# Column sums of a gate's normalisation: from a float32 product of 8 columns to a product of 16 split columns

## The chip, the cores and the metric

The kernel runs on one core of a Trainium2 chip. The metric is the device time of one execution in microseconds (us). The engines are PE (TensorE; its weight loads are listed apart, as PEld), DVE (VectorE), ACT (ScalarE), POOL (GpSimd) and SP (SyncE, which issues the transfers here).

## What is computed

Three stages follow one another: an attention through packed keys, a gated two-layer network, and a network of eight experts. The change lies in the weights that the third stage gives its experts. `P` has one row for each of 2304 tokens and one column for each of 8 experts; eight times its rows and then its columns are scaled to fixed sums.

```python
def _moe2_ref(x, w_gate, w1, w2):
    N, D = x.shape
    E = w_gate.shape[1]
    logits = x @ w_gate
    logits = logits - logits.max()
    P = np.exp(logits)
    for _ in range(8):
        P /= P.sum(1, keepdims=True) + 1e-09
        P /= P.sum(0, keepdims=True) + 1e-09
        P *= N / E
    out = np.zeros((N, D), dtype=np.float32)
    for e in range(E):
        h = np.maximum(x @ w1[e], 0.0)
        ye = h @ w2[e]
        out += P[:, e:e + 1] * ye
    return out
```

## The kernel before

The third stage is cut into groups of tokens. The first group has 256 tokens, and its work runs in 16 steps (two halves of the inner width for each expert), some 370 to 551 us into the span. While it runs, the normalisation is worked off beside it, in small pieces: `sinkhorn` (L1225) is a generator, and the loop of the first group (L1475) calls it once in each half step, behind the half step's second product. The order on PE, DVE and ACT is the order in which the code is written.

A step `s` has two halves, `j = 0` and `j = 1`, and each goes as follows. PE computes the first layer of half the inner width (`up0`: four wide products at L1026, four of 256 columns at L1029, and both once more; tile `u`). ACT copies a part of the result (L1035) and DVE adds the two parts (L1036, tile `us`). The result is split into a rounded part (ACT, L1042) and a rest (DVE, L1043, tile `h`). PE computes the second layer of the step before for 128 of the tokens (`down0`, L1058, 12 products of 512 columns, tile `d`). Beside that, weights are split in the same way: ACT rounds a block (L870), and DVE subtracts the rounded part from the raw one (L872), in j = 0 for the first layer of the next step (`w1l`), in j = 1 for the second layer of this step (`w2l`). Each split makes two blocks in a half. The second `w2l` block of a step is first read by the eighth of the 12 products of the following half, since the products take `w2h`, `w2l`, `w2h` for each of four pieces of the inner width and the second block starts with the third piece. A raw block is loaded anew once DVE has subtracted it.

An iteration of the normalisation takes two such pieces. Behind the half j = 0, DVE forms the row sums' reciprocals, scales `P`, and sums each column over the 18 tokens of a partition (L1269 to L1275, result `csum`, 128 partitions by 8). Behind the half j = 1, one product of `csum` with a matrix of ones adds up the partitions (L1278; all in float32; tile `cs`), and DVE adds a small constant, takes the reciprocal and scales `P` (L1280 to L1282), and then begins the next iteration's row sums (L1269). All eight iterations lie between 396 and 481 us. From the step of expert 4 on, DVE also adds up the weighted outputs (L1070, L1071, L1078), and in part of the stage it prepares the tokens of the second group (L976, L987).

Of the kernel before, what the change touches and what calls it, by code (L numbers as in the profile page):

```python
# [9 lines left out]
F32 = mybir.dt.float32  # L10
F32R = mybir.dt.float32r
# [3 lines left out]
ALU = mybir.AluOpType  # L15
AX = mybir.AxisListType
# [4 lines left out]
NE, FF2 = 8, 1024  # L21
# [5 lines left out]
EPS = 1e-9  # L27
# [77 lines left out]
def fused_kernel(  # L105
# [15 lines left out]
    pe, dve, act = nc.tensor, nc.vector, nc.scalar  # L121

    def pool(name, bufs, **kw):
        st = ExitStack()
        return st.enter_context(tc.tile_pool(name=name, bufs=bufs, **kw)), st

    const, _ = pool("const", 1, side="left"); ctx.enter_context(_)
# [24 lines left out]
    ones = const.tile([128, 128], F32, name="ones")  # L152
# [1072 lines left out]
    def sinkhorn():  # L1225
        lgs = {}
        for hh in (1, 0):
            ps = p3.tile([128, 512], F32, tag="y", name=f"lg{hh}")
            q0, nj, w = GATE[hh]
            for k in range(4):  # L1230
                for j in range(nj):
                    q = q0 + w * j
                    pe.matmul(ps[32 * j:32 * j + 32, :w], wg[:, k, :],  # L1233
                              x2[q // SB][k][:, q % SB:q % SB + w],
                              start=(k == 0), stop=(k == 3), tile_position=(0, 32 * j))
            lg = st["S"].tile([128, 2, 256], F32, tag="S", name=f"lgs{hh}").rearrange("p i n -> p (i n)")[:32 * nj, :w]
            dve.tensor_copy(lg, ps[:32 * nj, :w])
            lgs[hh] = lg
        yield
        Pt = const.tile([128, NE, 18], F32, name="P")  # L1240
        P = Pt.rearrange("p e t -> p t e")
        prob["P"] = P
        for hh in range(2):
            ps = p3.tile([128, 512], F32, tag="y", name=f"lt{hh}")
            q0, nj, w = GATE[hh]
            t0, nc_, m = q0 // 128, w // 128, 32 * nj
            for c in range(nc_):
                pe.transpose(ps[:, m * c:m * c + m], lgs[hh][:, 128 * c:128 * c + 128],
                             ident[:m, :m])
            dve.tensor_copy(  # L1250
                Pt[:, :, t0:t0 + nj * nc_].rearrange("p e (j c) -> p j c e", c=nc_),
                ps[:, :m * nc_].rearrange("p (c j e) -> p j c e", c=nc_, j=nj)[:, :, :, :NE])
        pm = const.tile([128, 1], F32, name="pm")
        dve.tensor_reduce(pm, Pt, AX.XY, ALU.max)
        yield
        ps = p3.tile([128, 512], F32, tag="y", name="gm")
        pe.transpose(ps[:1, :128], pm, ident)
        gm = const.tile([1, 1], F32, name="gmx")
        dve.tensor_reduce(gm, ps[:1, :128], AX.X, ALU.max, negate=True)
        yield  # L1260
        ps = p3.tile([128, 512], F32, tag="y", name="gb")
        pe.matmul(ps[:, :1], ones[:1, :], gm, start=True, stop=True)
        gb = const.tile([128, 1], F32, name="gb")
        dve.tensor_copy(gb, ps[:, :1])
        act.activation(Pt, Pt, AF.Exp, bias=gb)
        rsum = const.tile([128, 18], F32, name="rsum")
        csum = const.tile([128, NE], F32, name="csum")
        for it in range(8):
            dve.tensor_reduce(rsum, P, AX.X, ALU.add)  # L1269
            if it:  # L1270
                yield
            dve.tensor_scalar_add(rsum, rsum, EPS)
            dve.reciprocal(rsum, rsum)
            dve.tensor_tensor(P, P, rsum.unsqueeze(2).to_broadcast([128, 18, NE]), op=ALU.mult)
            dve.tensor_reduce(csum, Pt, AX.X, ALU.add)  # L1275
            yield
            ps = p3.tile([128, 512], F32, tag="y", name=f"cs{it}")
            pe.matmul(ps[:, :NE], ones, csum, start=True, stop=True)  # L1278
            rc = const.tile([128, NE], F32, tag="rc", bufs=2, name="rc")
            dve.tensor_scalar_add(rc, ps[:, :NE], EPS)  # L1280
            dve.reciprocal(rc, rc)
            dve.scalar_tensor_tensor(P, P, float(NT) / NE,  # L1282
                                     rc.unsqueeze(1).to_broadcast([128, 18, NE]),
                                     op0=ALU.mult, op1=ALU.mult)
        yield
        ps = p3.tile([128, 512], F32, tag="y", name="pt")
        Pf = Pt.rearrange("p e t -> p (e t)")
        pe.transpose(ps[:, :128], Pf[:, :128], ident)
        pe.transpose(ps[:16, 128:256], Pf[:, 128:], ident)
        t = st["cp"].tile([128, NB], F32, tag="cp", name="pts")  # L1290
        dve.tensor_copy(t[:, :128], ps[:, :128])
        dve.tensor_copy(t[:16, 128:256], ps[:16, 128:256])
        rows = pd.rearrange("e (t c) -> (e t) c", c=128)
        nc.sync.dma_start(rows[:128], t[:, :128])
        nc.sync.dma_start(rows[128:], t[:16, 128:256])
# [157 lines left out]

    with tc.manual_schedule(engines={mybir.EngineType.PE, mybir.EngineType.DVE, mybir.EngineType.Activation}):
        sk = sinkhorn()
        next(sk)
        for g in (1, 2):
# [116 lines left out]
```

## Time and profile before

| | before |
|---|---|
| time, median of 3 runs (lowest to highest) | 1777.64 us (1777.58 to 1777.78) |
| the profiled execution, its own time | 1776.45 us |
| span of the profiled execution | 1774.7 us |
| PE busy | 1760.6 us, 99% |
| PE weight loads busy | 1492.9 us, 84% |
| DVE busy | 1453.0 us, 82% |
| ACT busy | 1086.2 us, 61% |
| granted clock of TensorE | 1.00 of full speed |

The span is the time from the first instruction of the execution to the last; the device time contains 1.75 us more. The share of DVE is a mean over the whole span, and single stages lie far above it.

### The profile page before, as it was taken

Reading aid. Unit: us, or ns where it says so; the run is one execution under the profiler, and the core shown is the slowest. Engines: PE = TensorE matmul, PEld = TensorE weight load, DVE = VectorE, ACT = ScalarE, POOL = GpSimd, SP = SyncE. Lnnn points to the kernel's source line nnn. Section 1 sums busy time; section 2 is a strip of 40 time slices with the busy share of each in tenths; the row PEclk is TensorE's granted clock in tenths of the full one; section 3 lists DMA queues with packets and bytes.
Section 4 is the critical chain, followed back from the end, with each engine's and each line's share of the span. In section 5 each row is a group of like instructions: output and inputs, shape, how many; then the busy total and the mean of one; then the engine's idle time right before and its main releaser. Section 6 shows DMA issues by size and latency. Waiting matters only on the chain.

```text
span 1774.7 us, 24847 instructions
## 1 busy us (share of the span) xinstructions
PE 1760.6 (99%) x9320; PEld 1492.9 (84%) x9320; DVE 1453.0 (82%) x1954; ACT 1086.2 (61%) x1737; POOL 1.0 (0%) x8
## 2 busy tenths in 40 slices
PE   7999999999999999999999999999999999999999
PEld 5999999988888888888888888888888888888887
DVE  7968797668996989998889999887777777777778
ACT  6776675655664666656666666655555555555555
POOL 0000000000000000000000000000000000000000
PEclk9999999999999999999999999999999999999999
DMA  9326776866674755566454555955555444545442
GB/s 377 117 96 223 253 268 255 331 214 188 203 240 150 264 181 177 167 206 208 160 178 167 179 193 201 323 190 172 159 170 168 151 159 143 172 155 172 148 130 95
DMA packets 141000, 341.72 MB, mean 193 GB/s; under 512 B 11840, under 2 KB 49104, under 8 KB 139984
## 3 DMA queue, kind: packets, MB, share of 16 engines
q1 hardware_dynamic: 140880, 340.14, 56.8%
q8 instruction: 73, 1.20, 0.3%
q14 instruction: 47, 0.39, 0.1%
HBM read 256.66 MB, written 83.44 MB: 192 GB/s over the span
## 4 chain that ended last, share of the span: by engine, by line
PE 95%; DMA 2%; DVE 1%; ACT 1%; issue 0%; SPq 0%; DVEq 0%
PE d L1151 34%; PE X L1199 20%; PE Z L1199 10%; PE g2w L709 8%; PE g L616 5%; PE d L1058 5%; PE Y L1199 5%; PE u L1026 3%; PE g L672 3%; PE u L1029 2%; DMA kq<-in_kT_dram 2%; DMA rawout<-in_moe_w_out_dram 1%; PE u L194 1%; PE lg L1233 0%; DVE S L826 0%
## 5 line engine op out<-in xcount | busy, mean ns | idle before, releaser
L145 DVE TENSOR_TENSOR lo<-hb,hi 128x1024 fp32r<-128x1024 f32 x224 | 273.7, 1222 | 32.9 <-ACT hi L144 32.0
L1151 PE MATMUL d<-hi,w2f 128*128 128x512 f32 x896 | 294.2, 389 | 0.0
L1199 PE MATMUL X<-xf,w1l 128*128 128x512 f32 x1152 | 276.9, 389 | 0.0
L144 ACT CAST hi<-hb 128x1024 fp32r<-128x1024 f32 x224 | 235.3, 1051 | 66.7 <-PE d L1151 61.2
L1199 PEld LDWEIGHTS X<-xf,w1l 128*128 128x128 f32 x1152 | 216.2, 188 | 44.9
L1159 ACT COPY M<-d 128x512 f32<-128x512 f32 x235 | 137.9, 589 | 140.2 <-PE d L1151 139.0
L1163 DVE TENSOR_TENSOR M<-d,M 128x512 f32<-128x512 f32 x203 | 139.7, 688 | 99.9 <-PE d L1151 99.9
L1151 PEld LDWEIGHTS d<-hi,w2f 128*128 128x128 f32 x896 | 168.1, 188 | 34.9
L1151 PE MATMUL d<-lo,w2f 128*128 128x512 f32 x448 | 174.3, 389 | 0.0
L1151 PE MATMUL d<-hi,w2l 128*128 128x512 f32 x512 | 167.7, 389 | 0.0
L709 PE MATMUL g2w<-ring,woh 128*128 128x384 f32 x576 | 147.0, 335 | 0.2 <-DVE U L581 0.2
L1147 ACT COPY d<-M 128x512 f32<-128x512 f32 x217 | 127.7, 589 | 21.6 <-DVE M L1163 20.4
L1151 PE MATMUL d<-hi,w2g 128*128 128x512 f32 x384 | 125.7, 389 | 0.0
L1151 PEld LDWEIGHTS d<-hi,w2l 128*128 128x128 f32 x512 | 96.1, 188 | 20.2 <-ACT d L1147 0.4
L709 PEld LDWEIGHTS g2w<-ring,woh 128*128 128x128 f32 x576 | 102.9, 188 | 4.9 <-issue 3.4
L1206 ACT COPY cp<-X 128x512 f32<-128x512 f32 x128 | 74.5, 583 | 46.5 <-PE X L1199 46.4
L1151 PE MATMUL d<-lo,w2l 128*128 128x512 f32 x256 | 99.6, 389 | 0.0
L1151 PEld LDWEIGHTS d<-lo,w2f 128*128 128x128 f32 x448 | 84.1, 188 | 17.5
L1199 PE MATMUL Y<-xf,w1f 128*128 128x512 f32 x384 | 97.4, 389 | 0.0
L709 PE MATMUL g2w<-ring,wol 128*128 128x384 f32 x288 | 96.2, 334 | 0.0
L144 ACT CAST w1f<-rb 128x512 fp32r<-128x512 f32 x96 | 59.8, 624 | 56.7 <-PE d L1151 42.9
L1199 PE MATMUL Z<-xf,w1l 128*128 128x512 f32 x384 | 92.2, 389 | 0.0
(214 smaller groups left out, 3399.2 us busy)
## 6 DMA issues: line engine op xcount, KB each, us to landing
r<-in_moe_w_dram SPq DMA_DIRECT2D x128, 512.0 KB, 4.1
w1l<-w1d SPq DMA_DIRECT2D x128, 512.0 KB, 4.1
w1d<-po SPq DMA_DIRECT2D x64, 512.0 KB, 4.2
w2d<-w2f SPq DMA_DIRECT2D x64, 512.0 KB, 4.1
w2l<-w2d SPq DMA_DIRECT2D x64, 512.0 KB, 3.5
rb<-in_moe_w_dram SPq DMA_DIRECT2D x96, 256.0 KB, 2.7
sb<-in_moe_w_dram SPq DMA_DIRECT2D x48, 256.0 KB, 2.7
pb<-pd SPq DMA_DIRECT2D x16, 512.0 KB, 5.2
```

The source lines that it names most:

```text
L144: act.copy(out=hi, in_=raw)
L145: eng.tensor_tensor(out=lo, in0=raw, in1=hi.bitcast(F32), op=ALU.subtract)
L616: pe.matmul(ps, lhs[:, fs], rhs, start=(n == 0), stop=(n == 5))
L672: pe.matmul(ps[:, :HS], lhs, rhs, start=(n == 0), stop=(n == 3 * nf - 1))
L709: pe.matmul(ps[:, :TW], lhs[:, f % 2, ds], ring[f // 2][:, 2 * (f % 2) + rhs, q], start=(n == 0 and not on), stop=(n == 11), skip_group_ch ...
L1058: pe.matmul(ps, h[:, l, f % 2, 128 * tt:128 * tt + 128], w[:, f % 2], start=(fh == 0 and n == 0), stop=(fh == 1 and n == 11))
L1147: act.copy(out=ps, in_=m)
L1151: pe.matmul(ps, w[:, l, c, 128 * d:128 * d + 128], r[:, c], start=(n == 0 and not seed), stop=(n == 5), skip_group_check=seed)
L1159: act.copy(out=m, in_=ps)
L1163: dve.tensor_tensor(m, ps, m, op=ALU.add)
L1199: pe.matmul(ps, w[:, l, c, 128 * i:128 * i + 128], x[:, r, c], start=(n == 0 and p in (1, 7)), stop=(n == 5), skip_group_check=p in (2, 6, ...
L1206: act.copy(out=t, in_=ps)
```

## The change

`csum` is split in two: a rounded copy in the type float32r and the rest, both in one tile `cs2` of 16 columns. The matrix of ones is copied once into a float32r tile `onr`. The product then takes `onr` and the 16 columns, in the type in which the neighbouring products `u` and `d` run, and DVE adds the two halves of the result before the constant is added.

```diff
+        cs2 = const.tile([128, 2, NE], F32R, name="cs2")
+        onr = const.tile([128, 128], F32R, name="onr")
+        dve.tensor_copy(onr, ones)
         for it in range(8):
...
             dve.tensor_reduce(csum, Pt, AX.X, ALU.add)
+            dve.tensor_copy(cs2[:, 0], csum)
+            dve.tensor_tensor(cs2[:, 1], csum, cs2[:, 0].bitcast(F32), op=ALU.subtract)
             yield
             ps = p3.tile([128, 512], F32, tag="y", name=f"cs{it}")
-            pe.matmul(ps[:, :NE], ones, csum, start=True, stop=True)
+            pe.matmul(ps[:, :2 * NE], onr, cs2.rearrange("p l e -> p (l e)"), start=True, stop=True)
             rc = const.tile([128, NE], F32, tag="rc", bufs=2, name="rc")
-            dve.tensor_scalar_add(rc, ps[:, :NE], EPS)
+            dve.tensor_reduce(rc, ps[:, :2 * NE].rearrange("p (l e) -> p e l", l=2), AX.X, ALU.add)
+            dve.tensor_scalar_add(rc, rc, EPS)
             dve.reciprocal(rc, rc)
```

On DVE, the second iteration of the normalisation stands as follows before the change, from the column sums of `P` to the reciprocal (`us`, `h` and `w2l` belong to the half step between them):

```order
L1275 TENSOR_REDUCE csum<-P 128x8
L1036 TENSOR_TENSOR us_4817<-u_4800,us_4817 128x512
L872 TENSOR_TENSOR w2l_4794<-r_30_4713,w2h_4793 128x1024
L1043 SCALAR_TENSOR_TENSOR h_4826<-us_4817,h_4826 128x512
L872 TENSOR_TENSOR w2l_4824<-r_31_4736,w2h_4823 128x1024
L1280 TENSOR_SCALAR rc<-cs_4848 128x8
L1281 RECIPROCAL rc<-rc 128x8
```

And with the change (line numbers there are up to six higher):

```order
L1278 TENSOR_REDUCE csum<-P 128x8
L1279 CAST cs_4687<-csum 128x8
L1280 TENSOR_TENSOR cs_4687<-csum,cs_4687 128x8
L1036 TENSOR_TENSOR us_4825<-u_4808,us_4825 128x512
L872 TENSOR_TENSOR w2l_4800<-r_30_4718,w2h_4799 128x1024
L1043 SCALAR_TENSOR_TENSOR h_4834<-us_4825,h_4834 128x512
L872 TENSOR_TENSOR w2l_4832<-r_31_4741,w2h_4831 128x1024
L1285 TENSOR_REDUCE rc<-cs_4856 128x8
L1286 TENSOR_SCALAR rc<-rc 128x8
L1287 RECIPROCAL rc<-rc 128x8
```

Three instructions join each iteration, two ahead of `us` and one behind the second `w2l`; the order of the others stays. On PE the product keeps its place between the last product `d` of one half and the first product `u` of the next. Before:

```order
L1058 MATMUL d_4829<-w2h_4715,h_4718 128x512
L1278 MATMUL cs_4848<-csum,ones 128x8
L1026 MATMUL u_4855<-xs,w1h_4738 128x512 x2
```

And with the change:

```order
L1058 MATMUL d_4837<-w2h_4720,h_4723 128x512
L1283 MATMUL cs_4856<-cs_4687,onr 128x16
L1026 MATMUL u_4864<-xs,w1h_4743 128x512 x2
```

Only the product itself is another one. ACT, POOL and SP have the same instructions in the same order.

## Rows read from the trace of the kernel before

**Rows 1.** The page: span, busy time by engine, chain by engine.
```profile
span 1774.7 us, 24847 instructions
...
PE 1760.6 (99%) x9320; PEld 1492.9 (84%) x9320; DVE 1453.0 (82%) x1954; ACT 1086.2 (61%) x1737; POOL 1.0 (0%) x8
...
PE 95%; DMA 2%; DVE 1%; ACT 1%; issue 0%; SPq 0%; DVEq 0%
```

**Rows 2.** Chain that ended last: start us, us, engine, tile, line, instructions.
```profile
387.35 0.11 PE gm L1257
387.46 0.93 PE u L1026 x4
...
399.10 0.12 PE cs L1278 x2
...
410.43 0.12 PE cs L1278 x2
410.55 1.02 PE u L1026 x4
...
421.88 1.03 PE u L1026 x4
...
489.94 0.91 PE u L1026 x4
...
501.03 0.91 PE u L1026 x4
```

**Rows 3.** Instructions of L1278: count, shortest/median/longest ns, first and last start.
```profile
L1278 PEld LDWEIGHTS cs<-csum,ones x16: 188/188/189, 398.7 to 478.2; 128*128 128x128 f32 x16
L1278 PE MATMUL cs<-csum,ones x16: 172/214/256, 398.9 to 478.3; 128*128 128x8 f32 x16
```

**Rows 4.** Instructions of three DVE lines, columns as in Rows 3.
```profile
L1259 DVE TENSOR_REDUCE gmx<-gm x1: 273/273/273, 388.8 to 388.8; 1x1 f32<-1x128 f32 x1
...
L1275 DVE TENSOR_REDUCE csum<-P x8: 302/303/305, 397.8 to 475.3; 128x8 f32<-128x144 f32 x8
...
L1280 DVE TENSOR_SCALAR rc<-cs x8: 157/160/161, 401.5 to 480.2; 128x8 f32<-128x8 f32 x8
```

**Rows 5.** Timeline of DVE: start us, us, what, [idle before it <- what ended it].
```profile
396.37 0.41 DVE L1269 TENSOR_REDUCE rsum<-P 128x18 f32<-128x144 f32 x1 [1.82 <-ACT P L1265]
396.81 0.18 DVE L1272 TENSOR_SCALAR rsum<-rsum 128x18 f32<-128x18 f32 x1
...
397.79 0.30 DVE L1275 TENSOR_REDUCE csum<-P 128x8 f32<-128x144 f32 x1
398.01 0.68 DVE L1036 TENSOR_TENSOR us<-u,us 128x512 f32<-128x512 f32 x1
...
459.47 0.69 DVE L1036 TENSOR_TENSOR us<-u,us 128x512 f32<-128x512 f32 x1 [0.43 <-ACT us L1035]
...
465.00 0.69 DVE L1036 TENSOR_TENSOR us<-u,us 128x512 f32<-128x512 f32 x1 [0.20 <-ACT us L1035]
...
492.10 1.22 DVE L872 TENSOR_TENSOR w2l<-r,w2h 128x1024 fp32r<-128x1024 f32 x1
...
498.98 0.69 DVE L1036 TENSOR_TENSOR us<-u,us 128x512 f32<-128x512 f32 x1 [0.92 <-ACT us L1035]
```

**Rows 6.** Busy time in two steps: us, PE, PEld, DVE, ACT, POOL, clock, DMA, GB/s.
```profile
407.50:418.80 11.30, 11.30 (x60) 9.60 (x59) 9.27 (x17) 6.60 (x9) 0.00 (x0) 1.00 0.59 189
...
475.30:486.60 11.30, 11.30 (x60) 9.51 (x59) 11.09 (x18) 7.16 (x10) 0.00 (x0) 1.00 0.63 191
```

**Rows 7.** Timeline of PE: the eighth product of one half's 12.
```profile
494.18 0.40 PE L1058 MATMUL d<-w2l,h 128*128 128x512 f32 x1
```

**Rows 8.** Timeline of all engines, at the stage's end, columns as in Rows 5.
```profile
545.69 1.22 DVE L872 TENSOR_TENSOR w2l<-r,w2h 128x1024 fp32r<-128x1024 f32 x1
...
546.96 0.19 PEld L1058 LDWEIGHTS d<-w2l,h 128*128 128x128 f32 x1 [0.39 <-DVE w2l L872]
```

**Rows 9.** Waits of weight loads: who waited for whom, us in total, times, longest.
```profile
PEld d L1058 <- DVE w2l L872: 0.4, 1, 0.4
```

## The prediction

> **What bounds the kernel now.** I read the page first: PE is busy for 1760.6 of 1774.7 us, and 95% of the chain that ended last is PE's [rows 1]. So whatever shortens PE's own work counts in full, and whatever lies on DVE counts only where PE comes to wait for it. The chain in order of time then shows PE's work around the product that is changed. A step without it lasts 501.03 - 489.94 = 11.09 us, a step with it 421.88 - 410.55 = 11.33 us [rows 2]. One product, with all that it costs its neighbours, is therefore worth 0.24 us: 0.12 us under its own name, the rest in the first group of `u` behind it (1.02 us in place of 0.91) [rows 2]. The trace has 16 weight loads and 16 matmuls for the eight products, so each float32 product runs as two passes, each with a load of its own [rows 3]. The third view is DVE's. In a middle step of this stage it has 9.27 us of work in 11.30 us; in the step at 475 us it has 11.09 [rows 6], and from the wait of 0.20 us that ends at 465.00 to the one of 0.92 us that ends at 498.98 it never waits at all [rows 5]. Nearly the same engine load as PE's: this is the stretch in which added DVE work can be seen. The waits of the weight loads show that PE has come to wait for DVE's `w2l` once before, for 0.39 us, at 546.96 [rows 8, 9].
>
> **The change part by part.** *PE, removed.* A two-pass product of few columns costs 0.24 us, so a pass costs 0.12. A row for one pass alone is near: the product `gm` takes 0.11 us, and the `u` behind it 0.93 in place of 0.91, 0.13 in all [rows 2]; that one streams 128 columns, so its price is an upper one for 16. I take 0.12 for the single pass with 16 columns and 0.12 saved in each product, 8 x 0.12 = 0.96 us. The ends are nothing (if the new product costs what the old one did) and 8 x 0.24 = 1.92 us (if it vanished under its neighbours).
>
> *PE, a wait added?* The product now waits for two more DVE instructions. In the first iteration `csum` ends at 397.79 + 0.30 = 398.09 [rows 5] and the product stands in the chain from 399.10 [rows 2]; in the others DVE is done some microseconds ahead, as `csum` belongs to the half before. The two instructions take 0.39 us (next paragraph), so the sum is ready by 398.48. Nothing is queued late.
>
> *DVE, added.* A cast and a subtraction of 128x8 behind `csum`, and behind the product a reduction of 16 columns to 8 from PSUM. The tiny instructions have one row that is almost the same, the addition on 128x8 from PSUM, 160 ns; as upper neighbours there are reductions of 128 and 144 elements, 273 and 303 ns [rows 4]. Between dependent instructions there is a gap of 0.03 us (396.37 + 0.41 = 396.78 to 396.81), and an independent one begins some 0.08 us before the end of the one ahead of it (397.79 + 0.30 = 398.09 against 398.01) [rows 5]. Cast and subtraction, which depend on each other, push `us` back by 0.03 + 0.16 + 0.03 + 0.17 = 0.39 us, as the overlap at the end is there with and without them. The reduction I take at 0.18, between the addition and the longer reductions and nearer the addition, with its gap 0.21. Together e = 0.60 us for an iteration, on DVE 8 x 0.60 = 4.8 us. From both sides e is 0.45 (150 ns each, no gap) to 0.99 (three times 0.30 and a gap). The cast of the ones is one instruction, and it lies in DVE's wait of 1.82 us for the exponential [rows 5]; without that cover it would be one more 0.2 to 0.3 us on DVE, in a step where DVE has 2 us to spare.
>
> *Where DVE's cover ends.* In the middle steps the 11.30 - 9.27 = 2.03 us of idle time [rows 6] hide 0.60 and the 0.12 by which PE gets faster. For the last two iterations it is otherwise. I follow the lag of DVE behind PE, against before. The wait of 0.43 us that ends at 459.47 takes up the reduction and PE's gain of that step (0.21 + 0.12), so the lag is 0 there. The next wait is 0.20, and it has to cover cast and subtraction: 0.39 - 0.20 = 0.19 is left at 465.00. From there nothing is covered: PE's next gain 0.12, reduction 0.21, cast and subtraction 0.39, PE's last gain 0.12, reduction 0.21 make 1.24 us by the `w2l` at 492.10 [rows 5]. In letters this is 2e + 0.04.
>
> *What is late then.* That `w2l` is the second block of its step. It ends at 492.10 + 1.22 = 493.32, and its first reader is the eighth product of the half, at 494.18 [rows 5, 7]. A load can start 0.05 us after the end of the `w2l` it waits for (545.69 + 1.22 = 546.91 to 546.96) [rows 8], and needs some 0.12 us before its product starts (a pass, above). So there are 494.18 - 0.12 - 0.05 - 493.32 = 0.69 us of slack. A lag of 1.24 us exceeds it, and PE waits 1.24 - 0.69 = 0.55 us at that place. After it DVE's lag is down to the 0.69 that was slack, and the wait of 0.92 us that ends at 498.98 takes that up. A raw block is loaded anew when its `w2l` is done, so loads come later by the lag too, but none that PE's next half waits for.
>
> *The sum.* -0.96 + 0.55 = -0.41 us, in letters -0.96 + (2e + 0.04 - 0.69) = 2e - 1.61, with -0.96 as the floor. The profiled execution would go from 1776.45 to 1776.04 and its span from 1774.7 to 1774.3; the median of the runs shown is 1777.64, 1.19 above that execution, and becomes 1777.2. Behind the stage PE's chain goes on to the end, so I let what is gained stay gained.
>
> **The rivals.** *The cover holds.* If e is under 0.33, no wait arises, and the full 0.96 us come out: 1776.7. Against it stands the row of 160 ns for the smallest instruction; for it, that the slack is a difference of stamps of 0.1 us and that some added instructions may overlap. The Trainium skill, "VectorE: DVE Perf Modes", section on the TRN2 errata, gives a vector instruction 58 cycles from SBUF and 120 from PSUM at 0.96 GHz besides its elements: as an estimate by that page cast, subtraction and reduction take 0.07 + 0.07 + 0.14 = 0.28 us, and this rival would be the forecast. The 160 ns for 8 columns from PSUM [rows 4] are above the 133 ns that the same line gives.
>
> *DVE's additions cost more than PE's saving.* Place and mechanism are those of the forecast, the price of the instructions is the higher one. The sum turns at 2e = 1.61, that is at e = 0.81 us; at the upper bound of 0.99 it is +0.37 us: 1778.0. For it speak the reductions of 0.27 and 0.30 us [rows 4], against it that these read 128 and 144 elements where the new ones read 8 and 16.
>
> *The new product is no cheaper.* No row shows a product of 16 columns in float32r. If it costs the 0.24 us of the old one, PE saves nothing, and DVE's lag, now without PE's two gains of 0.12, is 1.00: a wait of 0.31 us, 1777.95.
>
> *Four passes go, not two.* Were the float32 product four passes long, each would be 0.06 us of the 0.24, and one pass would save 0.18: 1.44 us in eight. DVE's lag would be 1.24 + 2 x 0.06 = 1.36, the wait 0.67 and the sum -0.77: 1776.9. The records speak against it, two loads for each product [rows 3]. The Trainium skill, "FP8 and Floating Point Precision", section TensorE Precision Notes, says that true FP32 takes four passes through the array; the trace here shows two records, and the 0.24 us bound both readings.
>
> **How the numbers follow.** Chances: the forecast (some wait, a small gain, 1776.8 to 1777.5) 0.53, the cover holds 0.20, DVE costs more than PE saves 0.13, a product no cheaper 0.06, four passes 0.04, and 0.04 for something that no row shows. All named cases lie between 1776.7 and 1778.0. The executions before spread over 0.2 us among the timed ones, and the profiled one lies 1.2 us below them, so I add half a microsecond at either end: 1776.2 to 1778.5. A measurement of this kernel tells about 0.2% from no change, 3.6 us. Every named case is within that, so the chances are 0.02 faster, 0.96 the same and 0.02 slower, the outer ones for what no row shows.
>
> **What would show it.** The product `cs` appears with 8 loads and 8 matmuls in place of 16 and 16, and the step in the chain lasts 11.21 us in place of 11.33. Cast, subtraction and reduction appear on DVE with some 0.16 to 0.20 us each. Between 465 and 498 us DVE stays without a wait, and in the half at 493 us a weight load of `d` waits for a `w2l` by about half a microsecond. Wrong I would be if `cs` kept two passes, if no wait for `w2l` appeared at 493 us (then the gain is 0.96), if one appeared in other steps too, or if the span moved by more than 1 us either way with these stamps as forecast.

## The result and the profile after

The change made the kernel slower: 1797.81 us median (1797.51 to 1798.01, 4 runs) against 1777.61 us (1776.61 to 1777.78, 4 runs). The ratio is 1.0115 with an interval of 1.0097 to 1.0132: 20.2 us more, where 0.4 us less was forecast.

The page after, as in [rows 1]: span, busy time by engine.

```profile
span 1795.7 us, 24856 instructions
...
PE 1781.6 (99%) x9312; PEld 1489.8 (83%) x9312; DVE 1460.0 (81%) x1979; ACT 1087.6 (61%) x1737; POOL 1.0 (0%) x8
```

The span is 21.0 us longer, and PE is busy for 21.0 us more (1781.6 against 1760.6) although it has eight matmuls fewer. So this is no wait of PE for a neighbour: its own products take longer. The rest of this section looks first at the stage in which the change lies, and then for those products.

**The stage of the change.** The instructions of the product after (columns as in [rows 3]) and the four small ones on DVE that stand around it (as in [rows 4]):

```profile
L1283 PEld LDWEIGHTS cs<-cs,onr x8: 188/188/188, 398.6 to 476.8; 128*128 128x128 f32 x8
L1283 PE MATMUL cs<-cs,onr x8: 172/172/172, 398.8 to 477.1; 128*128 128x16 f32 x8
```

```profile
L1279 DVE CAST cs<-csum x8: 171/172/172, 398.0 to 475.0; 128x8 fp32r<-128x8 f32 x8
L1280 DVE TENSOR_TENSOR cs<-csum,cs x8: 166/168/169, 398.2 to 475.2; 128x8 fp32r<-128x8 f32 x8
L1285 DVE TENSOR_REDUCE rc<-cs x8: 165/166/168, 401.8 to 480.0; 128x8 f32<-128x16 f32 x8
L1286 DVE TENSOR_SCALAR rc<-rc x8: 171/172/173, 402.0 to 480.2; 128x8 f32<-128x8 f32 x8
```

Eight loads and eight matmuls stand in place of sixteen and sixteen. The chain in order of time (start us, us, engine, tile, line, instructions), as in [rows 2], ending with the first product of the stage behind:

```profile
387.27 0.11 PE gm L1257
...
410.15 0.01 PE cs L1283
410.17 1.03 PE u L1026 x4
...
421.34 1.03 PE u L1026 x4
...
550.31 2.74 PE X L1199 x12
```

A step with the product lasts 421.34 - 410.17 = 11.17 us in place of 11.33. DVE and PE at the place where the forecast saw its wait, first two instructions of the timeline, then the row of the waits (us in total, times, longest; the other of the two is the one of [rows 9]):

```profile
492.11 1.22 DVE L872 TENSOR_TENSOR w2l<-r,w2h 128x1024 fp32r<-128x1024 f32 x1
...
493.38 0.19 PEld L1058 LDWEIGHTS d<-w2l,h 128*128 128x128 f32 x1 [0.79 <-DVE w2l L872]
```

```profile
PEld d L1058 <- DVE w2l L872: 1.2, 2, 0.8
```

The new wait is there, at 493.38. From the product `gm` to the first product of the next stage, the stage takes 550.31 - 387.27 = 163.04 us, against 551.15 - 387.35 = 163.80 before (the first start in each difference is that of `gm`, the other that of the row `X` of the same chain; the one of before is shown next).

**Behind the stage.** The chain of before behind 551 us, where PE works off group after group of twelve products of 512 columns without a pause (`X`, `Y`, `Z` at L1199 for the first layer, `d` at L1151 for the second):

```profile
551.15 2.72 PE X L1199 x12
...
573.14 2.72 PE d L1151 x12
...
586.51 2.72 PE Z L1199 x12
```

The same pieces after:

```profile
566.65 2.72 PE Z L1199 x12
...
572.32 2.80 PE d L1151 x12
...
585.97 2.74 PE Z L1199 x12
```

The first group behind the stage, at 550.31, takes 2.74 us; behind it and up to 572 us the pace is that of before, 2.72 us for twelve products. With the first group of L1151 it becomes 2.80, and from there on L1199 takes 2.74. The program has 2688 products of either line (896 of them are the form `d<-hi,w2f` alone): 2688 / 12 x 0.08 = 17.9 us at L1151 and 2688 / 12 x 0.02 = 4.5 us at L1199, 22.4 us in all; the ends of the spans give 1795.7 - 550.31 = 1245.4 against 1774.7 - 551.15 = 1223.6 us, 21.8 more. With the 0.8 us gained by 550 us that is the 21.0 of the span. The windows of before and after show that it is neither the clock nor idle time (window, its length, busy time of PE, PEld, DVE, ACT, POOL with instructions, granted clock, DMA share, GB/s):

```profile
700.00:900.00 200.00, 200.00 (x884) 165.62 (x883) 178.00 (x237) 126.76 (x201) 0.00 (x0) 1.00 0.54 179
```

```profile
700.00:900.00 200.00, 200.00 (x868) 162.32 (x868) 174.24 (x231) 124.56 (x197) 0.00 (x0) 1.00 0.51 178
```

Granted clock 1.00 in both, PE busy throughout in both, and in 200 us 868 products where there were 884. DVE, ACT and the transfers have less to do after, since PE is late with everything.

No instruction of these lines is touched by the change. What it does touch is the memory. The trace has no addresses, so this goes by the order in the program: `cs2` (64 bytes in each partition) and `onr` (512 bytes) are two new tiles in the pool of constants, which lies first at the low end of SBUF. All tiles that are laid out behind it from this end (the weights `w1l`, `w2f`, the tokens `xf`) stand 576 bytes higher than before; those laid out from the other end (`hi`, `lo`, `xs`) stand where they stood. L1151 loads the weights `w2f` and streams `hi` and `lo`: its two operands come from the two ends. That was the first theory: the distance between them has changed, and the product's pace with it. Its rivals: the new instructions themselves, through the order or the transfers, or the lost cover on DVE.

### The profile page after: what moved, and what is told of

Same layout as the page of the kernel before. It is cut to its first block, busy times and chain, and to the rows that moved or that the text cites. A ratio compares the mean times of both kernels' runs of the same rounds, so it can differ in the third digit from the quotient of the medians.

```text
span 1795.7 us, 24856 instructions
## 1 busy us (share of the span) xinstructions
PE 1781.6 (99%) x9312; PEld 1489.8 (83%) x9312; DVE 1460.0 (81%) x1979; ACT 1087.6 (61%) x1737; POOL 1.0 (0%) x8
## 4 chain that ended last, share of the span: by engine, by line
PE 96%; DVE 2%; DMA 2%; ACT 0%; issue 0%; SPq 0%; DVEq 0%; ACTq 0%
PE d L1151 34%; PE X L1199 19%; PE Z L1199 9%; PE g2w L709 8%; PE g L616 6%; PE Y L1199 5%; PE d L1058 5%; PE u L1026 3%; PE g L672 3%; PE u L1029 2%; PE u L194 1%; DMA kq<-in_qT_dram 1%; DMA rawin<-in_moe_w_in_dram 0%; DMA r<-in_moe_w_dram 0%; PE lg L1233 0%; PE s L194 0%
## 5 line engine op out<-in xcount | busy, mean ns | idle before, releaser
L1151 PE MATMUL d<-hi,w2f 128*128 128x512 f32 x896 | 299.2, 394 | 0.0
L1199 PE MATMUL X<-xf,w1l 128*128 128x512 f32 x1152 | 278.7, 390 | 0.0
L1199 PEld LDWEIGHTS X<-xf,w1l 128*128 128x128 f32 x1152 | 216.2, 188 | 48.2
L1151 PEld LDWEIGHTS d<-hi,w2f 128*128 128x128 f32 x896 | 167.6, 187 | 40.5
L1151 PE MATMUL d<-lo,w2f 128*128 128x512 f32 x448 | 176.5, 394 | 0.0
L1151 PE MATMUL d<-hi,w2l 128*128 128x512 f32 x512 | 170.6, 394 | 0.0
L1151 PE MATMUL d<-hi,w2g 128*128 128x512 f32 x384 | 127.8, 394 | 0.0
L1151 PEld LDWEIGHTS d<-hi,w2l 128*128 128x128 f32 x512 | 95.8, 187 | 23.4 <-ACT d L1147 0.3
L1151 PE MATMUL d<-lo,w2l 128*128 128x512 f32 x256 | 100.9, 394 | 0.0
L1151 PEld LDWEIGHTS d<-lo,w2f 128*128 128x128 f32 x448 | 83.9, 187 | 19.9
L1199 PE MATMUL Y<-xf,w1f 128*128 128x512 f32 x384 | 98.0, 391 | 0.1
L1199 PE MATMUL Z<-xf,w1f 128*128 128x512 f32 x384 | 92.9, 390 | 0.0
```

The costliest lines, as they stand in the source:

```text
L1151: pe.matmul(ps, w[:, l, c, 128 * d:128 * d + 128], r[:, c], start=(n == 0 and not seed), stop=(n == 5), skip_group_check=seed)
L1199: pe.matmul(ps, w[:, l, c, 128 * i:128 * i + 128], x[:, r, c], start=(n == 0 and p in (1, 7)), stop=(n == 5), skip_group_check=p in (2, 6, ...
```

## The experiments

**The shift alone.** The kernel before, with one unused tile of the same size:

```diff
         csum = const.tile([128, NE], F32, name="csum")
+        const.tile([128, 144], F32, name="pad")
```

> The kernel before, with one tile of 576 bytes per partition declared behind csum in the pool of constants and never used: no instruction is added, only the tiles of the left side of SBUF (the blocks of weights w2f and w1l, the tokens xf) lie 576 bytes higher, as they do with the change. Theory of the place (the lost 20 us come from where the tiles lie): about 1798 us, twelve products of tile d at L1151 take 2.80 us in place of 2.72, and the column sums' product stays as before at 0.24 us. Rival, the arithmetic (the new product, or DVE's additions, slow something later): 1777.6 us, no change.

Measured: 1797.19 us (1797.12 to 1797.84, 4 runs) against 1777.57, ratio 1.0111 (1.0096 to 1.0126). Its chain:

```profile
572.31 2.80 PE d L1151 x12
...
585.95 2.74 PE Z L1199 x12
```

The whole loss is there without a single changed instruction.

**The change without the shift.** The same arithmetic, laid out so that the pool of constants keeps its size: the matrix of ones itself is float32r, and three tiny tiles share one.

```diff
-    ones = const.tile([128, 128], F32, name="ones")
-    nc.gpsimd.memset(ones, 1.0)
+    ones = const.tile([128, 128], F32R, name="ones")
...
+        dve.tensor_scalar(ones, ident, 0.0, 1.0, op0=ALU.mult, op1=ALU.add)
...
-        onr = const.tile([128, 128], F32R, name="onr")
-        dve.tensor_copy(onr, ones)
+        onr = ones
```

> The changed kernel with the same split and the same single product, but without a byte more in the pool of constants: the ones are written once as float32r by DVE and serve both products, and three one-column tiles share one. The tiles of the left side lie where they lay before the change. Theory of the place: the forecast's own sum comes out, 1776.6 to 1777.4 us, with one wait for w2l near 493 us of about half a microsecond and 2.72 us for twelve products at L1151. Rival, the arithmetic: about 1797.8 us as the change.

Measured: 1776.99 us (10 runs) against 1777.57, ratio 0.9996 (0.9987 to 1.0005). The loss is gone, and what is left can't be told from no change. A gain of 0.4 us, as forecast, lies within the interval, and so does none.

**Another shift.** The change with 448 unused bytes more among the constants, so that everything laid out from that end is shifted by 1024:

> The changed kernel with 448 more unused bytes in the pool of constants, so that the left side lies 1024 bytes higher than before the change. Theory of the place, in the form that it is the address within a kilobyte (or less) that counts: 1776.6 to 1777.4 us. In the form that any move away from the old place costs: about 1798. Rival, the arithmetic: about 1797.8.

Measured: 1776.64 us (10 runs), ratio 0.9996 (0.9987 to 1.0006). More bytes, and no loss: it isn't the amount of memory. `d` at L1151 has 2.72 us for twelve again.

**The other end moved too.** The change as it is, and 448 unused bytes at the other end, which put `hi`, `lo` and the rest there 448 bytes lower. The distance has then grown by 576 + 448 = 1024.

```diff
     const, _ = pool("const", 1, side="left"); ctx.enter_context(_)
+    rp, _ = pool("rp", 1, side="right"); ctx.enter_context(_)
+    rp.tile([128, 112], F32, name="rpad")
```

> The changed kernel with 448 unused bytes at the upper end of SBUF, so that the tiles of the right side (hi, lo, hb, xs, h) lie 448 bytes lower, and stand to the tiles of the left side as before the change up to a multiple of 1024. If only the distance of the two operands of a product counts: products at L1151 back to 2.72 us for twelve, those at L1199, both of whose operands lie on the left, still at 2.74, together about 1781 us. If each operand's own place counts: L1151 between 2.74 and 2.80 us for twelve, 1785 to 1798 us. Rival, the arithmetic: about 1797.8.

Measured: 1776.95 us (10 runs), ratio 0.9997 (0.9988 to 1.0007). The left-hand tiles stand where they stand after the change, and the loss is gone: the distance decides, not the place. The expectation was wrong in one point: it left L1199 at 2.74 us and the time at 1781, as both operands of L1199 stand 576 bytes higher. L1199 went back to 2.72 us as well, so what it had lost after the change came from L1151's slow groups and not from its own operands.

**Which distances.** The kernel before with unused bytes among the constants, one run each:

> The kernel before with 64 unused bytes in the pool of constants. If the distance of a product's two operands counts within 512 bytes, this is the same as 576 bytes: products at L1151 2.80 us for twelve, about 1797.5 us. If it counts within more than 512 bytes (1024, say), the pace may be another: 2.72 to 2.80. If the number of bytes counts as such, about 1780 us.

> The kernel before with 128 unused bytes in the pool of constants. If every distance but a multiple of 512 costs the same: 2.80 us for twelve products at L1151, about 1797.5 us. If the loss is a matter of how two streams of reads meet, it is another number here, between 2.60 and 2.95 us for twelve, 1750 to 1830 us.

> The kernel before with 256 unused bytes in the pool of constants: half of 512, the farthest from the old distance. If every distance but a multiple of 512 costs the same: 2.80 us for twelve, about 1797.5. If the loss is a matter of how two streams of reads meet: another number, between 2.60 and 2.95 us for twelve, 1750 to 1830 us.

> The kernel before with 448 unused bytes in the pool of constants, the mirror of 64 within 512. If the sign of the distance doesn't count: as with 64 bytes, about 1797.5 us. If it does: another pace at L1151, between 2.60 and 2.95 us for twelve.

Measured beside 1776.75 for the kernel before: 64 bytes 1797.32, 128 bytes 1796.54, 256 bytes 1777.67, 448 bytes 1797.63 us. The single tile of 64 bytes costs 20 us. 448 bytes cost as much, but the loss is shared out otherwise:

```profile
613.14 2.76 PE d L1151 x12
...
621.21 2.77 PE X L1199 x12
```

L1151 takes 2.76 us and not 2.80, and L1199, both of whose operands moved together, takes 2.77 and not 2.74: here the line whose own distance is unchanged loses more than the one whose distance changed.

Fast were 0, 256 and 1024. From this came the rule that shifts by multiples of 256 bytes leave the pace as it was (576 is 2 x 256 + 64), and it was tried on four shifts that had not run:

> The kernel before with 512 unused bytes per partition among the constants. Theory (only the distance between the loaded and the moving tile of a product counts, and multiples of 256 bytes of shift leave the pace as it was): 1776 to 1778 us, and twelve products of d at L1151 in 2.72 us. Rival (any shift but the two found fast costs 20 us): 1797 us, 2.80.

> The change with 192 more unused bytes, so that the shift is 768 bytes, three times 256. Theory of multiples of 256: 1776 to 1778 us, twelve products in 2.72 us, w2l wait of 0.6 to 0.8 us at 493 us. Rival (only powers of two are fast): 1797 us, 2.80.

> The kernel before with 64 unused bytes at the other end of SBUF: the tiles hi, lo, hb, xs, gh and acc are 64 bytes lower, the tiles at the left end (constants, w2f, w1l, xf) stand where they stood. Theory (distance of the two operands): as slow as 64 bytes on the left, 1797 us, twelve products of L1151 in 2.80 us. Rival (the place of the left-hand tiles themselves is what counts): 1777 us, 2.72.

> The kernel before with 32 unused bytes among the constants, the smallest tile that the pool lays out apart. Theory (any distance that is not a multiple of 256 is slow): 1797 us, twelve products in 2.80 us. Rival (what matters is measured in units of 64 bytes, so that half a unit changes nothing, or only part of it): 1777 us or a time between, 2.72 to 2.80.

Measured beside 1777.00 for the kernel before: 512 bytes 1776.49, the change with a shift of 768 bytes 1776.71, 64 bytes at the other end 1797.30, 32 bytes 1800.63 us. All four as the rule has it, and 32 bytes, half the smallest slow shift seen before, cost no less. (It is one run, 3.3 us above that with 64 bytes; the 25 executions of the kernel before, run beside the first four experiments, lie between 1776.28 and 1780.91 us.) The change with 768 bytes of shift, and so without the loss, is also the cleanest look at what was forecast; its chain:

```profile
387.57 0.11 PE gm L1257
...
550.96 2.72 PE X L1199 x12
```

From `gm` to the next stage it takes 550.96 - 387.57 = 163.39 us, 0.41 less than before's 163.80. (After the change as it is, 0.76 less: part of that is the shift's own doing, which changes the pace of the stage's products too. The kernel before with 64 unused bytes takes 163.35 us there.)

**TensorE alone.** What was still open is whether the two operands of one product are at odds with each other, or PE's reads with those of another engine or of the transfers, which shift against them as well. A kernel of its own, which does nothing of the reference's work, runs the form of L1151 on tiles of zeros, 96 products in a row for each of nine placements, and that four times: alone, beside DVE, beside ACT, beside transfers.

> Not the reference's work: products of zeros in the form of L1151 (float32r, 128x512, a load for each), 96 in a row for each of nine placements, first alone (tiles pa to pk), then beside a stream of subtractions on DVE (va to vk), of copies on ACT (sa to sk) and of transfers into SBUF (ta to tk). Loaded tile shifted by 0, 32, 64, 128, 192, 256, 448 bytes (letters a, b, c, e, f, g, i), moving tile by 64 (j), both by 64 (k). Theory (a product's own two operands): already alone, a, g and k go at 0.227 us for a product, the others at 0.230 to 0.235. Rival (TensorE's reads meet another engine's): alone all nine go at the same pace, and only beside DVE, ACT or the transfers they differ. Second rival (products alone go faster than 0.227 everywhere): the pace of a, g and k is itself set by the neighbours.

Its chain. The first letter of a tile is the neighbour (`p` none, `v` DVE, `s` ACT, `t` transfers), the second the shift of the loaded tile: a 0, b 32, c 64, e 128, f 192, g 256, i 448 bytes; j is the moving tile by 64, k both by 64.

```profile
53.50 21.77 PE pa L65 x96
75.26 22.39 PE pb L65 x96
97.66 22.40 PE pc L65 x96
120.05 22.31 PE pe L65 x96
142.36 21.98 PE pf L65 x96
164.34 21.77 PE pg L65 x96
186.11 21.98 PE pi L65 x96
208.09 22.00 PE pj L65 x96
230.09 21.77 PE pk L65 x96
251.86 21.78 PE va L65 x96
...
296.03 22.40 PE vc L65 x96
...
450.23 21.78 PE sa L65 x96
...
494.40 22.40 PE sc L65 x96
...
648.60 21.78 PE ta L65 x96
...
692.77 22.40 PE tc L65 x96
```

Alone, a product takes 21.77 / 96 = 0.2268 us at a, g and k, and 22.40 / 96 = 0.2333 at c: the two paces of L1151, 2.72 / 12 = 0.227 and 2.80 / 12 = 0.233. 448 bytes go as 192 (448 - 256), the moving tile by +64 as the loaded one by 192 (-64 + 256), and both by 64 as none. Beside a stream of subtractions on DVE, of copies on ACT or of transfers, the same placements take the same time to 0.02 us in 22. The rivals of other engines are out: the two paces are there without them, and they follow the distance between PE's loaded and its moving tile, modulo 256 bytes. Which load and which stream meet isn't shown. By the starts in the trace a load begins 2 to 4 ns after the start of the product ahead of its own (tile `pf`), so it may be a product's load and the stream of the product ahead of it that count; within a group all products have the same distance, and the runs don't tell the two readings apart. The nearest reading is that TensorE's two reads, load and stream, stand in each other's way; no run shows that directly.

**The other line.** In the shifts so far, L1199, whose two operands (`w1l` loaded, `xf` streamed) both come from the low end, never changed its own distance. 64 bytes between the two do that, and leave L1151's operands alone:

```diff
     wp, _ = pool("wp", 16, side="left"); ctx.enter_context(_)
+    xp, _ = pool("xp", 1, side="left"); ctx.enter_context(_)
+    xp.tile([128, 16], F32, name="xpad")
```

> The kernel before with 64 unused bytes behind the pool of the weights: the tiles xf, cp and pb stand 64 bytes higher; w1l, w2f and all tiles of the right end stand where they stood. Theory (a product's own two operands): the slow products are those of L1199, whose moving tile is xf, from the first group behind 551 us on: 2.76 to 2.80 us for twelve in place of 2.72, and L1151 is slow at most as an after-effect; 2688 products by 2 to 7 ns, 1782 to 1797 us. Rival (accesses of other engines): L1199 and L1151 stay at 2.72, 1777 us.

Measured: 1794.78 us beside 1777.23. Its chain (L1201 and L1153 are the lines L1199 and L1151 there):

```profile
551.13 2.76 PE X L1201 x12
...
562.14 5.49 PE X L1201 x24
...
573.35 2.75 PE d L1153 x12
...
589.66 2.77 PE d L1153 x12
```

Now L1199 is slow from its first group on, before any product of L1151 has run: 5.49 / 24 = 0.2288 us, the 21.98 / 96 = 0.2290 of the small kernel for this distance. And L1153, whose own distance is the old one, takes 2.75 to 2.77: a part of the pace is passed on from the group before. The expectation gave it that only as an after-effect; it is as large as the cause here: over the whole stage a product takes 230.3 ns at L1201 and 230.0 at L1153, by the starts in the trace (226.7 at either before). Of the twelve products of a group of L1153, the pace settles at 226.7 ns, on average, only with the last two, and it is the same with the groups of L1199 in the kernel with 448 bytes. After the change it was the other way round, 0.02 us for L1199 as after-effect of L1151's 0.08: there the second to the fifth product take 235.8, 228.3, 232.5 and 230.8 ns on average, the others 226 to 227. So the small kernel, where a placement stays for 96 products, doesn't give the price in a kernel in which the two lines take turns. For 448 bytes its 229.0 in place of 226.8 ns would make 2688 x 2.2 ns = 5.9 us; the kernel lost 20.9. In the small kernel the after-effect is seen at a change of placement, where the first few products of a fast group still take 229 to 233 ns by the starts in the trace (tile `pg`: 229, 232, 231, then 227).

## Why the prediction was wrong, point by point

**The product**, -0.12 us in each step: right. With the shift of 1024 bytes, which leaves the pace of the neighbours alone, the step is 11.22 us, forecast 11.21:

```profile
398.88 1.02 PE u L1026 x4
...
410.09 0.01 PE cs L1284
410.10 1.02 PE u L1026 x4
```

From 398.88 to 410.10; what is left of the product is paid nearly whole by the `u` behind it: 0.01 us under its own name and 0.11 there (1.02 in place of 0.91), 0.12 together as forecast. The row of `gm`, which the forecast set beside its 0.12, splits it the other way, 0.11 and 0.02.

**DVE's additions**, e = 0.60 us: right. Cast 0.172, subtraction 0.168, reduction 0.166; the addition, now from SBUF, takes 0.172 where it took 0.160. With three gaps of 0.03 that is 0.61. The rival by the cycle table of the Trainium skill, "VectorE: DVE Perf Modes", section on the TRN2 errata, an estimate of 0.07 + 0.07 + 0.14 us, is refuted by these rows: each of the three takes about 0.17 us, from SBUF as from PSUM.

**Where DVE's cover ends, and what is late then**: right in place and mechanism, with the wait some 0.1 us shorter than forecast. The wait is the load of `d` for the `w2l` of the half at 493 us, on the same product and no other new one. DVE's waits after:

```profile
452.84 0.69 DVE L1036 TENSOR_TENSOR us<-u,us 128x512 f32<-128x512 f32 x1 [0.38 <-ACT us L1035]
498.31 0.69 DVE L1036 TENSOR_TENSOR us<-u,us 128x512 f32<-128x512 f32 x1 [0.24 <-ACT us L1035]
```

Nothing stands between: the waits of 0.43 and 0.20 us of [rows 5] are used up (the forecast left 0.10 of the first), and of the 0.92 there 0.24 is left, 0.68 taken up, as the slack of 0.69 had it. What PE lost by its wait is read best without the loss, in the change with 768 bytes of shift. From the sixth product of the half to the ninth, PE before and then there:

```profile
493.72 0.62 PE L1058 MATMUL d<-w2h,h 128*128 128x512 f32 x2
494.18 0.40 PE L1058 MATMUL d<-w2l,h 128*128 128x512 f32 x1
494.42 0.62 PE L1058 MATMUL d<-w2h,h 128*128 128x512 f32 x2
```

```profile
493.09 0.62 PE L1058 MATMUL d<-w2h,h 128*128 128x512 f32 x2
493.90 0.50 PE L1058 MATMUL d<-w2l,h 128*128 128x512 f32 x1 [0.19 <-DVE w2l L872]
494.24 0.63 PE L1058 MATMUL d<-w2h,h 128*128 128x512 f32 x2
```

Three products take 494.24 - 493.09 = 1.15 us in place of 494.42 - 493.72 = 0.70: the wait costs 0.45 us, where 0.55 was forecast (0.47 with 1024 bytes, 0.45 with none).

**The sum of the stage**, -0.41 us: the runs agree with it, as far as single executions tell. With shifts that are multiples of 256 bytes, or none, the changed kernels take 163.39 (768 bytes), 163.39 (1024), 163.45 (none) and, with both ends moved, 163.55 us from `gm` to the first `X`; the unchanged ones 163.80 (none), 163.86 (512) and 164.25 (256). The middle values, 163.42 and 163.86, lie 0.44 apart, but the three unchanged ones are spread over 0.45, so that the match to a hundredth is luck. None of the rivals named decided anything.

**What failed** is the sentence behind the sum: "Behind the stage PE's chain goes on to the end, so I let what is gained stay gained." And, ahead of it, the list of parts itself. It costed each instruction that the diff adds, removes or moves, and it left out that two of the added lines are tiles: 576 bytes in a pool in front of everything that is laid out from the same end. The price of that term is 17.9 + 4.5 us by the chain, 2688 products by 6.7 ns and as many by 1.7, and it lies in a stage that the prediction had not looked at, since no instruction of it was changed. With no such case among the rivals, the range ended at 1778.5 and the chance of slower was 0.02; the 0.04 for what no row shows was far too little for a change that moves addresses. The prediction's own last sign of being wrong is what came: the span moved by more than 1 us with the stamps as forecast. The trace of before could not price the term, as it shows one distance only. It could have shown the stake: 84% load work beside 99% product work on PE [rows 1], that is, two streams of reads for most of the time, and a stage of 1220 us in which PE's pace is the time.

## What to carry to other kernels

A tile that is added or grows moves every tile laid out behind it from the same end, so in a kernel that TensorE bounds it belongs on the list of parts like an instruction; look which products take their loaded and their moving operand from different sides of it, and count the products that come behind those too. When a small change costs much more than its instructions, run the old kernel with unused bytes of the same size first: one run tells layout from work, and filling up the difference to a multiple of 256 bytes gave the 20 us back here. The change itself is then worth some 0.4 us of its stage by single executions, too little to be told from nothing in the total (0.9996, 0.9987 to 1.0006).

## What the runs showed of the hardware that was not expected

A float32r product of 512 columns with a weight load of its own takes 226.8 ns from start to start, the pace of the kernel before, where loaded and moving tile stand as in placement a of the small kernel or 256 bytes farther apart, and 228.9 to 233.3 at the other distances tried (32 and 64 bytes more 233, 128 bytes 232.4, 192 bytes 229.0), at a granted clock of 1.00 and with nothing else running. 32 bytes differ from none, so the unit is no larger than that. Neither whole multiples of 256 bytes nor the neighbours' traffic made a difference. Some of a slow pace is passed on to the products that follow, for about three products in the small kernel, and in the whole kernel up to the fifth of a group of twelve after the change, and up to the tenth with 448 bytes and in the last experiment.

Open is why: no record shows which of the two reads gives way, which load meets which stream, how a slow pace is passed on, or what is counted in 256 bytes. Open is also whether 32 bytes cost more than 64 in the whole kernel (3.3 us by one run each), when the small kernel shows the two alike (22.39 and 22.40 us): 1.9 us of it lie in the stage of the first group, which takes 165.25 us from `gm` to the first `X` with 32 bytes and 163.35 with 64. Other forms of products were not tried alone.
